# A gated attention/MLP mix on one core: no block and no closing barrier, two gate sums at another place, one output store on another queue

## The chip, the cores and the metric

One core of one Trainium2 chip runs the whole program. The metric is the device time of one launch in microseconds (us), median of several runs; less is better.

## The reference

The input `x` has 2048 rows (positions) of 512 numbers in bfloat16. Two branches are mixed by a gate that is one number per row:

```python
g = sigmoid((x * gate_w).sum(-1, keepdims=True))
# branch A: attention with 32 heads of width 16 over 8 positions, 2 apart
qkv = x @ wqkv
idx = pos[:, None] - 2 * arange(8)[None, :]          # masked where < 0
logits = einsum("bhsd,bhswd->bhsw", q, k[idx]) * 16 ** -0.5
a = einsum("bhsw,bhswd->bhsd", softmax(logits), v[idx]).reshape(B, S, D) @ wo
# branch B: an MLP over the positions
h = layernorm(B_x)
u = gelu(einsum("bsd,sf->bdf", h, w1) + b1)          # F = 1792
b = (einsum("bdf,fs->bds", u, w2) + b2).transpose(0, 2, 1)
out = g * a + (1 - g) * b
```

The kernel uses `x` for both branches and for the gate.

## The kernel before

The kernel is written as a list of named operations. Each has an engine, a function that issues its instructions, an assumed duration, and the tiles that it reads and writes. A list scheduler (`_Sched.schedule`) puts each engine's operations in an order, from assumed durations and dependences, and `plan_waits` gives each operation the semaphore waits that it needs. Where the author wants a certain order, `chain([...])` (near L932) fixes the sequence of the named operations on their engine. Afterwards `emit_engine` (L974 to L994) issues one engine's operations with their waits. At the end of SyncE's list (engine name `sp`) it also waits for the landing of every output store, semaphore by semaphore (L994).

All this stands in `nc.Block()` (L335). A block gives every engine an instruction stream of its own: each engine branches from the main body into its stream (L996 to L1012), and at the end of the block each branches to a common end, where all five engines meet at a barrier. That barrier's instructions carry line 335 in the profile. Ahead of the block, the main body holds four constant fills and an opening barrier (L1028).

The stages that matter here, by engine:

- TensorE (PE): ten warm-up matmuls (L526); the projections to q, k and v (L594); the sums of q times k over the head width (`qkr`, L672); the MLP's first product (`ph2`, L786) and second product (`ph3`, L836); and the product with `wo` (L852). TensorE's list ends with `ph3b_14`, `wo_0` to `wo_3`, `ph3a_15`, `ph3b_15`, then `wo_4` to `wo_15`. The last four output tiles are done in halves of 256 columns.
- VectorE (DVE): layernorm statistics (L549); the products q times k (`qkm`, L664); the 16 gate sums `gz_0` to `gz_15` (L648), each one product with an accumulated sum over one tile of 128 rows; the mask (`msk`, L712); the softmax (`sm_*`, L718 to L751); the products of the attention weights with v and their sums over 8 positions (`avm`, `ava`, `avb`, `avc`: L771, L774, L776); and the final combination of an output tile (`cmb_i`, L873), which reads the `wo` product from PSUM, multiplies it by the gate and adds branch B.
- ScalarE (ACT): evictions of the projections (L602, L605) and of the logits (`lev`, L702), the normalisation (L573), the softmax's exponential (`sm_exp0` and `sm_exp1`, L737), the gelu (L807), the bias copies `b1c` and `b2c` (L517, L518), and branch B's eviction (L903). It also issues 32 transfers that spread the attention weights over the partitions.
- SyncE (SP): issues nearly all other transfers. Tile `i` of the output is stored by `d_out<i>`; tile 15 is stored in halves, the first by SyncE (`d_out15a`) and the second by ScalarE (`d_out15b`, semaphore `d_outb`).

VectorE's order around the softmax is written out by hand. Before the change it is: `gz_12` to `gz_15`, `msk_0`, `sm_ma0`, `sm_mb0`, `gz_0`, `gz_1`, `msk_1`, `sm_ma1`, `sm_mb1`, `sm_m1`, `sm_sub0`, `sm_sub1`, the ten operations from `sm_sa0` to `sm_nrm1`, `gz_2` to `gz_11`, and then `avm_0`. `msk_1` waits for ScalarE's last `lev`; `sm_sa0` waits for `sm_exp0`.

Of the kernel before, what the change touches and what calls it, by code (L numbers as in the profile page):

```python
# [13 lines left out]
D = 512  # L14
# [4 lines left out]
NST = S // 128  # L19
# [313 lines left out]

def bass_gated_mix__sliding_local_dilated__mixer_token_mlp__prompt_kernel(nc, A_x, A_wqkv, A_wo, B_x, B_w1, B_b1, B_w2, B_b2, gate_w, out, dbg=None):
    with contextlib.ExitStack() as es:  # L335
        block = es.enter_context(nc.Block())
        view, pview, off, total = _views(nc, es)
        ps = es.enter_context(nc.psum_tensor("ps", [128, 8, 512], FP32))
        esem = {e: es.enter_context(nc.semaphore("sem_" + e)) for e in ("pool", "act", "dve", "pe")}
        sch = _Sched()  # L340
# [6 lines left out]
        outv = out[0].rearrange("(t p) d -> p t d", p=128)  # L347
# [21 lines left out]
        T1 = view("X", BF16, [(D, NST), (1, D)])  # L369
# [33 lines left out]
        def col(v_, i):  # L403
            return bass.AP(v_.tensor, v_.offset + i, [list(v_.ap[0]), [1, 1]])
# [24 lines left out]
        def mk_dma(dst, src):  # L429
            return lambda e: e.dma_start(dst, src)  # L430
# [115 lines left out]
        for hf in range(2):  # L546
            t0 = 8 * hf
            for t in range(t0, t0 + 8):
                A("dve", (lambda t_: (lambda e: e.bn_stats(out=ST6[:, t_, :], in_=X[:, t_, :])))(t), 0.59,  # L549
                  reads=["x%d" % t], writes=["st6_%d" % t], name="ln1_%d" % t, prio=0)  # L550
# [13 lines left out]
              reads=["zc%d" % hf], writes=["sd%d" % hf], name="ln_sqrt%d" % hf, prio=0)  # L564
            A("dve", (lambda t0_: (lambda e: e.reciprocal(out=cols(RSTD, t0_, 8), in_=cols(SD, t0_, 8))))(t0), 0.25,
              reads=["sd%d" % hf], writes=["rstd%d" % hf], name="ln_rstd%d" % hf, prio=0)
# [43 lines left out]
        for (b0, d0, d1, s0, s1) in ((0, 0, 1, 0, 512), (0, 1, 2, 0, 512), (0, 2, 3, 0, 512), (0, 3, 4, 0, 512), (4, 0, 2, 0, 512), (4, 2, 4, 0, 512)):  # L610
            for b in range(b0, b0 + 4):
                tn, dl = first[b]
                last_main[0] = A("pe", f_proj(tn, dl, 0, b, d0, d1, s0, s1), 0.216 * (d1 - d0) * (s1 - s0) / 512,
                                 reads=ALLXT[s0 // 128:s1 // 128] + ["wqkv%d_%d" % (tn, dt) for dt in range(d0, d1)],
# [11 lines left out]
        for (tn, dl, sb) in seq_proj:  # L626
# [3 lines left out]
                             reads=xr + ["wqkv%d_%d" % (tn, dt) for dt in range(4)],  # L630
# [15 lines left out]
        for t in range(NST):  # L646
# [7 lines left out]
          reads=["th"], writes=["g"], name="g_g", prio=0)  # L654
        A("dve", lambda e: e.tensor_scalar(out=OMG, in0=TH, scalar1=-0.5, scalar2=0.5, op0=ALU.mult, op1=ALU.add), 0.15,
          reads=["th"], writes=["omg"], name="g_omg", prio=0)
        A("dve", lambda e: e.tensor_tensor(out=C2, in0=OMG, in1=B2C, op=ALU.mult), 0.15,
          reads=["omg", "b2c"], writes=["c2"], name="g_c2", prio=0)
# [25 lines left out]
        for wh in range(2):  # L684
# [6 lines left out]
            for (dl, c0, nc_) in pieces:  # L691
# [3 lines left out]
                  reads=["q5_%d_%d" % (dl, sb) for sb in range(c0, c0 + nc_)] +  # L695
# [3 lines left out]
            for wl in range(4):  # L699
                qop = A("pe", f_qkr(list(enumerate(bufs)), (wl,)), 0.92, reads=rd, writes=["lg%d_0" % (4 + wl), "lg%d_1" % (4 + wl)],  # L700
                        name="qkr_%d_%d" % (wh, wl), prio=-100 + wl, delay=BURST_DELAY)
                A("act", (lambda wh_, wl_: (lambda e: e.activation(out=ATT[:, :, 4 * wh_ + wl_, :], in_=ps[:, 4 + wl_, :].rearrange("p (h c) -> p h c", h=2), func=AF.Copy)))(wh, wl),  # L702
                  0.55, reads=["lg%d_0" % (4 + wl), "lg%d_1" % (4 + wl)], writes=["lw%d" % (4 * wh + wl)],
                  name="lev_%d_%d" % (wh, wl), prio=0)
# [24 lines left out]
        for hf in range(2):  # L729
# [3 lines left out]
              reads=["outs1"], writes=["lh%d" % hf] + (wall if hf == 0 else []), name="sm_sub%d" % hf, prio=0)  # L733
            if hf == 0:
                A("act", lambda e: e.activation(out=col(SD, 0), in_=col(ZC, 0), func=AF.Exp, scale=0.0), 1.5,
                  reads=["zc0"], writes=["sd0"], name="sm_pre")
            A("act", (lambda hf_, l_: (lambda e: e.activation(out=ATT[:, hf_], in_=l_, func=AF.Exp)))(hf, lgh), 1.95,  # L737
              reads=["lh%d" % hf], writes=["att%d" % hf], name="sm_exp%d" % hf, prio=0)
        for hf in range(2):
# [5 lines left out]
            def f_rcp(e, hf_=hf):  # L745
# [6 lines left out]
              reads=["rs%d" % hf], writes=["att%d" % hf], name="sm_nrm%d" % hf, prio=0)  # L752
# [4 lines left out]
        for u in range(8):  # L757
            c, hf = u // 2, u % 2
            ds_at = sch.dsem("atx%d" % u)
            for a_ in range(4):  # L760
                dst = bass.AP(ATX.tensor, ATX.offset + a_ * pst + u * NW * HC, [[4 * pst, 32], [1, NW * HC]])
                sch.dma("act", mk_dma(dst, psub(ATT, 32 * c, 32, hf * NW * HC, [(1, NW * HC)])), 32 * NW * HC * 2, ds_at, issue=0.62,
                        reads=["att%d" % hf], writes=["atx_%d_%d" % (u, a_)], deps=pb_readers, name="d_atx_%d_%d" % (u, a_))
        USEQ = [0, 2, 1, 3, 4, 6, 5, 7]
        for k_, u in enumerate(USEQ):
# [6 lines left out]
              reads=v_res + ["atx_%d_%d" % (u, a_) for a_ in range(4)], writes=[pn] + [qk_res, k_all][k_ % 2], name="avm_%d" % u)  # L772
# [30 lines left out]
        for ft in range(NFT):  # L803
# [5 lines left out]
              reads=["acc%d" % bank, "b1c"], writes=["ut%d" % ft] + ALLXT,  # L809
              name="gel_%d" % ft, prio=0)  # L810
# [30 lines left out]
        def WB(i):  # L841
            return (4 + i) % 8

        def WBN(i):
            b_ = WB(i)
            return ["acc%d" % b_] if b_ < 4 else ["lg%d_0" % b_, "lg%d_1" % b_]

        def f_wo(i, bank, c0=0, c1=D):
            def fn(e):
                ins = None  # L850
                for t in range(4):
                    ins = e.matmul(ps[:, bank, 0:c1 - c0], lhsT=OT[:, t, 128 * i:128 * i + 128], rhs=WO[:, t, c0:c1],  # L852
                                   start=(t == 0), stop=(t == 3))
                return ins
            return fn

        ds_out = [sch.dsem("out%d" % k) for k in range(4)]
        ds_outb = sch.dsem("outb")
# [3 lines left out]
        def emit_wo(i):  # L862
            parts = [(0, D)] if i < HT0 else [(0, D // 2), (D // 2, D)]
            ons = []
            for h, (c0, c1) in enumerate(parts):
                k_ = i if len(parts) == 1 else HT0 + 2 * (i - HT0) + h
                bank, bn = WB(k_), WBN(k_)
                sfx = "" if len(parts) == 1 else "ab"[h]
                frac = (c1 - c0) / D
                on = "o%d%s" % (i, sfx)  # L870
                ons.append(on)
                A("pe", f_wo(i, bank, c0, c1), 0.866 * frac, reads=["ot%d" % (i // 2), "wo"], writes=bn, name="wo_%d%s" % (i, sfx), prio=0)
                A("dve", (lambda i_, b_, c0_, c1_: (lambda e: e.scalar_tensor_tensor(  # L873
                    out=T1[:, i_, c0_:c1_], in0=ps[:, b_, 0:c1_ - c0_], scalar=col(G, i_), in1=T1[:, i_, c0_:c1_],
                    op0=ALU.mult, op1=ALU.add)))(i, bank, c0, c1), 0.08 + 0.67 * frac, reads=bn + ["g", "t1_%d" % i], writes=[on],
                  name="cmb_%d%s" % (i, sfx), prio=0)
                if i == NST - 1:
                    q = "act" if sfx == "b" else "sp"
                    sch.dma(q, mk_dma(outv[:, i, c0:c1], T1[:, i, c0:c1]), 128 * (c1 - c0) * 2,
                            ds_out[i % 4] if q == "sp" else ds_outb, issue=0.5, reads=[on], name="d_out%d%s" % (i, sfx))  # L880
            if i < NST - 1:
                sch.dma("sp", mk_dma(outv[:, i, :], T1[:, i, :]), 128 * D * 2, ds_out[i % 4], issue=0.5, reads=ons, name="d_out%d" % i)

        p3bank = {}

# [8 lines left out]
        for i in range(NST):  # L894
# [4 lines left out]
            elif i > 1:  # L899
# [5 lines left out]
              reads=["acc%d" % bank, "omg", "c2"], writes=["t1_%d" % i, "x%d" % i],  # L905
              name="t1_%d" % i, prio=0)
            if i % 2 == 1 and j2 + 3 <= 7:
                ld_w2(j2 + 3)
        for i in range(NST):
            emit_wo(i)  # L910
# [15 lines left out]
        def gz(*ts):  # L926
            return ["gz_%d" % t for t in ts]

        def lnr(hf):
            return ["ln_rstd%d" % hf, "ln_nmr%d" % hf]  # L930
# [1 line left out]
        chain(["rp"] + ln1(0, 1, 2, 3) + ["qkm_0_0_0", "qkm_0_1_0"] + ln1(4, 5, 6, 7) + ln2(0)  # L932
              + ["qkm_0_2_0"] + lnr(0) + ["qkm_0_3_0", "qkm_0_0_2"] + ln1(8, 9) + ["qkm_0_1_2", "qkm_0_2_2", "qkm_0_3_2"] + ln1(*range(10, 16)) + ln2(1)
              + ["t_b", "qkm_1_0_0"] + lnr(1) + ["qkm_1_1_0"]
              + ["qkm_1_2_0", "qkm_1_3_0"] + gz(12, 13, 14, 15) + ["msk_0", "sm_ma0", "sm_mb0"] + gz(0, 1) + [
                 "msk_1", "sm_ma1", "sm_mb1", "sm_m1", "sm_sub0", "sm_sub1"]
              + ["%s%d" % (n_, h_) for h_ in range(2) for n_ in ("sm_sa", "sm_sb", "sm_s1", "sm_rcp", "sm_nrm")] + gz(*range(2, 12))
              + ["%s_%d" % (n_, u) for k_ in range(4) for n_ in ("avm", "ava", "avb", "avc") for u in USEQ[2 * k_:2 * k_ + 2]] + ["cmb_%d" % i for i in range(HT0)] + ["cmb_%d%s" % (i, x_) for i in range(HT0, NST) for x_ in "ab"])
        byname["d_w1_6"].deps.add(byname["d_atx_2_3"])
        chain(["d_w1_3", "d_xb", "d_gw", "d_xa", "d_w1_4", "d_w2_0", "d_w2_1", "d_w1_5", "d_w1_6", "d_w2_2"])  # L940
# [27 lines left out]
        def emit_engine(eng_name, e):  # L968
            for op in sch.order[eng_name]:
                for d in op.waits:  # L970
                    if d.is_dma:
                        e.wait_ge(d.dsem.handle, 16 * d.seq)
                    else:
                        e.wait_ge(esem[d.eng], d.seq)  # L974
                r = op.fn(e)
                if dbg is not None:
                    rr = r[-1] if isinstance(r, list) else r
                    dbg.setdefault("opmap", []).append((eng_name, op.name, rr.ins.name, op.start, op.end))
                if op.is_dma:
                    r.then_inc(op.dsem.handle, 16)  # L980
                elif op.sig:
                    if isinstance(r, list):
                        r = r[-1]
                    r.then_inc(esem[eng_name], 1)
            if eng_name == "sp" and dbg is not None and "keep" in dbg:
                for d in sch.dsems:
                    n_ = len([o for o in sch.ops if o.is_dma and o.dsem is d])
                    if n_ and d.queue == "sp":
                        e.wait_ge(d.handle, 16 * n_)
            if eng_name == OUTQ:  # L990
                for d in ds_out + [ds_outb]:
                    n_ = len([o for o in sch.ops if o.is_dma and o.dsem is d])
                    if n_:
                        e.wait_ge(d.handle, 16 * n_)  # L994

        @block.sync  # L996
        def _(e):
            emit_engine("sp", e)

        @block.gpsimd  # L1000
        def _(e):
            emit_engine("pool", e)

        @block.scalar
        def _(e):
            emit_engine("act", e)

        @block.vector
        def _(e):
            emit_engine("dve", e)  # L1010

        @block.tensor  # L1012
        def _(e):
            emit_engine("pe", e)


# [26 lines left out]
```

## Time and profile before

| | before |
|---|---|
| median of 3 runs | 169.39 us (169.17 to 169.87) |
| profiled execution, its own time | 169.05 us |
| span of the profiled execution, first to last instruction | 167.3 us |
| TensorE busy | 163.2 us |
| VectorE busy | 150.6 us |
| ScalarE busy | 74.7 us |

The span goes from the first instruction of the program to the end of the last one. The execution's own time is longer, since it has the launch around it. In the profile's views, `PEld` is TensorE's weight load, and a `q` behind an engine's name is its sequencer, which waits, branches and issues transfers while the engine may be idle. Matmuls are pipelined, so the busy time of one overlaps that of the next; the time from one start to the next is what a matmul costs.

### The profile page before, as it was taken

What the parts mean: (1) busy time and instruction counts of PE and PEld (TensorE: products, weight loads), DVE (VectorE), ACT (ScalarE), POOL (GpSimd) and SP (SyncE); (2) the same over time, 40 slices, a digit from 0 to 9 for tenths busy, and PEclk for the clock granted to TensorE, in tenths of its full rate; (3) what the DMA queues carried; (4) which work ended last, traced back from release to release, by engine and by line L of the source; (5) the groups of instructions that cost most, each with busy time, mean ns of one, the idle gap of its engine ahead of it and who ended that gap; (6) DMA issues with size and microseconds to landing.
All of it is one profiled execution on the core that took longest, in us unless ns stands there. A gap on an engine that the chain in (4) does not pass through costs nothing.

```text
span 167.3 us, 2153 instructions
## 1 busy us (share of the span) xinstructions
PE 163.2 (98%) x858; PEld 77.6 (46%) x858; DVE 150.6 (90%) x153; ACT 74.7 (45%) x115; POOL 0.7 (0%) x8
## 2 busy tenths in 40 slices
PE   7899999999999999999999999999999999999993
PEld 3455555554554444444444444444444444444462
DVE  0046999998999997799999999999999999999994
ACT  3087698889799818791122311231321312211000
POOL 1000000000000000000000000000000000000000
PEclk9999999999999999999999999999999999999999
DMA  6999999968004856996689926372574370000464
GB/s 149 304 271 258 305 322 290 310 203 233 0 0 122 287 160 164 305 290 148 142 216 338 347 70 156 89 218 83 138 219 126 95 222 0 0 0 0 158 206 142
DMA packets 47609, 29.64 MB, mean 177 GB/s; under 512 B 9840, under 2 KB 46448, under 8 KB 47600
## 3 DMA queue, kind: packets, MB, share of 16 engines
q1 hardware_dynamic: 45776, 25.11, 54.2%
q10 hardware_dynamic: 1824, 4.39, 9.6%
q8 instruction: 7, 0.11, 0.3%
q14 instruction: 2, 0.02, 0.0%
HBM read 21.11 MB, written 2.10 MB: 139 GB/s over the span
## 4 chain that ended last, share of the span: by engine, by line
DVE 57%; PE 35%; DMA 3%; ACT 2%; issue 1%
PE ps L594 25%; DVE arena L771 21%; DVE arena L774 16%; DVE arena L873 7%; PE ps L786 6%; PE ps L672 4%; DVE arena L718 4%; DVE arena L648 4%; DMA arena<-in_A_x_dram 3%; DVE arena L747 2%; DVE arena L776 2%; DVE arena L751 1%; ACT arena L737 1%; DVE arena L732 1%; ACT arena L702 0%
## 5 line engine op out<-in xcount | busy, mean ns | idle before, releaser
L786 PE MATMUL ps<-arena 128*128 128x512 bf16 x224 | 48.7, 379 | 0.0
L836 PE MATMUL ps<-arena 128*128 128x512 bf16 x224 | 48.7, 379 | 0.0
L594 PE MATMUL ps<-arena 128*128 128x512 bf16 x192 | 41.8, 379 | 0.6 <-DMA arena<-in_A_x_dram 0.6
L664 DVE TENSOR_TENSOR arena<-arena 128x4096 bf16<-128x4096 bf16 (+1 forms) x12 | 35.5, 2996 | 1.9 <-ACT arena L605 1.4
L771 DVE TENSOR_TENSOR arena<-arena 128x8192 bf16<-128x8192 bf16 x8 | 35.0, 4419 | 0.0
L786 PEld LDWEIGHTS ps<-arena 128*128 128x128 bf16 x224 | 21.8, 98 | 26.6 <-ACT arena L702 0.4
L836 PEld LDWEIGHTS ps<-arena 128*128 128x128 bf16 x224 | 21.9, 98 | 26.5
L594 PEld LDWEIGHTS ps<-arena 128*128 128x128 bf16 x192 | 21.6, 113 | 20.7 <-issue 1.0
L903 ACT ACTIVATE arena<-ps,arena 128x512 bf16<-128x512 f32 x16 | 12.4, 778 | 39.4 <-PE ps L836 39.4
L774 DVE TENSOR_TENSOR arena<-arena 128x4096 bf16<-128x4096 bf16 (+1 forms) x16 | 27.0, 1751 | 0.0
L605 ACT ACTIVATE arena<-ps 128x512 bf16<-128x512 f32 x32 | 18.6, 596 | 4.7 <-PE ps L594 4.7
L807 ACT ACTIVATE arena<-ps,arena 128x512 bf16<-128x512 f32 x14 | 9.6, 687 | 22.0 <-PE ps L786 15.7
L549 DVE BATCH_NORM_STATS2 arena<-arena 128x6 f32<-128x512 bf16 x16 | 10.0, 680 | 9.1 <-DMA arena<-in_A_x_dram 9.1
L852 PE MATMUL ps<-arena 128*128 128x512 bf16 (+1 forms) x80 | 14.2, 337 | 0.0
L602 ACT ACTIVATE arena<-ps 128x512 bf16<-128x512 f32 x16 | 9.0, 596 | 7.4 <-PE ps L594 7.3
L573 ACT ACTIVATE arena<-arena 128x512 bf16<-128x512 bf16 x16 | 12.2, 807 | 0.0
L873 DVE SCALAR_TENSOR_TENSOR arena<-ps,arena 128x512 bf16<-128x512 f32 (+1 forms) x20 | 11.2, 634 | 0.0
L852 PEld LDWEIGHTS ps<-arena 128*128 128x128 bf16 x80 | 7.8, 98 | 6.2
L648 DVE SCALAR_TENSOR_TENSOR arena<-arena 128x512 bf16<-128x512 bf16 x16 | 10.0, 686 | 0.0
L718 DVE TENSOR_TENSOR arena<-arena 128x512 bf16<-128x512 bf16 (+4 forms) x11 | 7.3, 667 | 1.2 <-ACT arena L737 0.8
L672 PE MATMUL ps<-arena 128*32 128x512 bf16 x128 | 7.3, 380 | 0.0
L702 ACT ACTIVATE arena<-ps 128x512 bf16<-128x512 f32 x8 | 4.7, 593 | 4.6 <-PE ps L672 4.6
(38 smaller groups left out, 39.2 us busy)
## 6 DMA issues: line engine op xcount, KB each, us to landing
arena<-in_B_w_dram SPq DMA_DIRECT2D x7, 1024.0 KB, 8.4
arena<-in_B_w_dram SPq DMA_DIRECT2D x8, 896.0 KB, 5.1
arena<-arena ACTq DMA_DIRECT2D x32, 128.0 KB, 2.9
arena<-in_A_x_dram SPq DMA_DIRECT2D x4, 512.0 KB, 5.3
out_dram<-arena SPq DMA_DIRECT2D x15, 128.0 KB, 1.7
arena<-in_A_x_dram SPq DMA_DIRECT2D x1, 1536.0 KB, 8.1
arena<-in_A_wqkv_dram SPq DMA_DIRECT2D x2, 256.0 KB, 3.6
arena<-in_A_x_dram SPq DMA_DIRECT2D x2, 256.0 KB, 3.6
```

The lines of the kernel that those rows point to most:

```text
L594: ins = e.matmul(ps[:, bank, s0:s1], lhsT=lhsT, rhs=XT[:, dt, sb * 512 + s0:sb * 512 + s1], start=(dt == 0 and s0 == 0), stop=(dt == 3))
L605: return lambda e: e.activation(out=dst, in_=ps[:, bank, :], func=AF.Copy)
L648: A("dve", (lambda s_, t_: (lambda e: e.scalar_tensor_tensor(out=s_, in0=s_, scalar=1.0, in1=GWB, op0=ALU.mult, op1=ALU.mult, accum_out=co ...
L664: return lambda e: e.tensor_tensor(out=PBL[buf][:, :, 512 * c0:512 * (c0 + nc_)], in0=in0, in1=in1, op=ALU.mult)
L672: ins = e.matmul(ps[32 * c:32 * c + 32, 4 + wl, :], lhsT=RP, rhs=PBL[buf][:, wl, c * 512:(c + 1) * 512], start=(dl == 0), stop=(dl == 3), ...
L718: return A("dve", lambda e: e.tensor_tensor(out=o_, in0=a_, in1=b_, op=op_), dur, reads=rd, writes=wr, name=nm)
L771: A("dve", (lambda o_, i0, i1: (lambda e: e.tensor_tensor(out=o_, in0=i0, in1=i1, op=ALU.mult)))(pv, in0, in1), 4.4, reads=v_res + ["atx_% ...
L774: A("dve", (lambda pv_, n__: (lambda e: e.tensor_tensor(out=pv_[:, 0:n__], in0=pv_[:, 0:n__], in1=pv_[:, n__:2 * n__], op=ALU.add)))(pv, n ...
L786: ins = e.matmul(ps[:, bank, :], lhsT=W1W[:, slot, st, 128 * e_:128 * e_ + 128], rhs=X[:, st, :], start=(st == 0), stop=(st == NST - 1))
L836: ins = e.matmul(ps[:, bank, :], lhsT=W2S[slot][:, ft, 128 * e_:128 * e_ + 128], rhs=UT[:, ft, :], start=(ft == 0), stop=(ft == NFT - 1))
L852: ins = e.matmul(ps[:, bank, 0:c1 - c0], lhsT=OT[:, t, 128 * i:128 * i + 128], rhs=WO[:, t, c0:c1], start=(t == 0), stop=(t == 3))
L873: A("dve", (lambda i_, b_, c0_, c1_: (lambda e: e.scalar_tensor_tensor(out=T1[:, i_, c0_:c1_], in0=ps[:, b_, 0:c1_ - c0_], scalar=col(G, i ...
```

## The change

Four things change.

1. `nc.Block()` is gone. All engines' instructions are issued into the main body, after the opening barrier. So the five branches into the block, the branches out of it, and the barrier at its end are gone. SyncE's waits for the output stores stay; they are now the last instructions of the program. The semaphore of SyncE's last wait was carried by the branch out of the block; it now stands on a wait of its own kind, in another pairing: `d_out2`, then `d_out3` with `d_out1`, then `d_outb` with `d_out0`.
2. `gz_2` moves from behind the softmax to the place just ahead of `msk_1`, and `gz_3` to the place between `sm_sub1` and `sm_sa0`.
3. The store of output tile 14 is issued by ScalarE instead of SyncE. It shares the semaphore `d_outb` with the second half of tile 15, ahead of which it stands in ScalarE's order.
4. As the scheduler's assumed times shift, it also puts ScalarE's copy `b1c` (L517) later: behind the fourth `lev` of the first group instead of between two projection evictions.

Nothing that is computed changes, and TensorE's order stays as it was.

```diff
-        block = es.enter_context(nc.Block())
...
             if i < NST - 1:
-                sch.dma("sp", mk_dma(outv[:, i, :], T1[:, i, :]), 128 * D * 2, ds_out[i % 4], issue=0.5, reads=ons, name="d_out%d" % i)
+                q = "act" if i == NST - 2 else "sp"
+                sch.dma(q, mk_dma(outv[:, i, :], T1[:, i, :]), 128 * D * 2, ds_out[i % 4] if q == "sp" else ds_outb, issue=0.5, reads=ons, name="d_out%d" % i)
...
-              + ["qkm_1_2_0", "qkm_1_3_0"] + gz(12, 13, 14, 15) + ["msk_0", "sm_ma0", "sm_mb0"] + gz(0, 1) + [
-                 "msk_1", "sm_ma1", "sm_mb1", "sm_m1", "sm_sub0", "sm_sub1"]
-              + ["%s%d" % (n_, h_) for h_ in range(2) for n_ in ("sm_sa", "sm_sb", "sm_s1", "sm_rcp", "sm_nrm")] + gz(*range(2, 12))
+              + ["qkm_1_2_0", "qkm_1_3_0"] + gz(12, 13, 14, 15) + ["msk_0", "sm_ma0", "sm_mb0"] + gz(0, 1, 2) + [
+                 "msk_1", "sm_ma1", "sm_mb1", "sm_m1", "sm_sub0", "sm_sub1"] + gz(3)
+              + ["%s%d" % (n_, h_) for h_ in range(2) for n_ in ("sm_sa", "sm_sb", "sm_s1", "sm_rcp", "sm_nrm")] + gz(*range(4, 12))
...
-        @block.sync
-        def _(e):
-            emit_engine("sp", e)
...
-        @block.tensor
-        def _(e):
-            emit_engine("pe", e)
+        for eng_name, e in (("sp", nc.sync), ("pool", nc.gpsimd), ("act", nc.scalar), ("dve", nc.vector), ("pe", nc.tensor)):
+            emit_engine(eng_name, e)
```

More of the change, by code (lines that the diff above doesn't have):

```diff
@@ L994, in emit_engine @@
                         e.wait_ge(d.handle, 16 * n_)
-        @block.sync
-        def _(e):
-            emit_engine("sp", e)
-        @block.gpsimd
-        def _(e):
[L1002 to L1010, printed above, removed]
-        @block.tensor
-        def _(e):
-            emit_engine("pe", e)
+        for eng_name, e in (("sp", nc.sync), ("pool", nc.gpsimd), ("act", nc.scalar), ("dve", nc.vector), ("pe", nc.tensor)):
+            emit_engine(eng_name, e)
 _INS = ['A_x', 'A_wqkv', 'A_wo', 'B_x', 'B_w1', 'B_b1', 'B_w2', 'B_b2', 'gate_w']
```

## The prediction

> **What bounds the kernel now.** I read the page first: span, busy times, and the chain that ended last.
>
> ```profile
> span 167.3 us, 2153 instructions
> ...
> PE 163.2 (98%) x858; PEld 77.6 (46%) x858; DVE 150.6 (90%) x153; ACT 74.7 (45%) x115; POOL 0.7 (0%) x8
> ...
> DVE 57%; PE 35%; DMA 3%; ACT 2%; issue 1%
> ```
>
> The two lines disagree. By busy time TensorE (PE) is full; by the chain, VectorE (DVE) carries 57% of the span. The chain is followed back from the last busy instruction and stays on an engine as long as that engine had no gap, so it names one tight path, not the only one. I therefore asked for busy time by stage (columns: length; PE, weight load, DVE, ACT, POOL; clock; DMA), and for TensorE's own rows of the timeline.
>
> ```profile
> 5.10:154.10 149.00, 148.93 (x784) 70.20 (x785) 139.16 (x133) 72.64 (x113) 0.00 (x0) 1.00 0.65 179
> 154.10:164.70 10.60, 10.58 (x65) 6.16 (x63) 10.60 (x20) 0.78 (x1) 0.00 (x0) 1.00 0.47 158
> ```
>
> ```profile
> 147.64 3.62 PE L852 MATMUL ps<-arena 128*128 128x512 bf16 x16
> ...
> 154.11 10.56 PE L852 MATMUL ps<-arena 128*128 128x512 bf16 x64
> ```
>
> ```profile
> L852 PE MATMUL ps<-arena 128*128 128x512 bf16 x48 | 10.7, 379 | 0.0
> ```
>
> ```profile
> 60.82 3.60 PE ps L672 x64
> ```
>
> Busy matmuls overlap, so 148.93 of 149.00 does not yet say full rate. The timeline does: 16 matmuls in 3.62 us, of which the last one's own length is 0.38 (379 ns, by its group's row), make (3.62 - 0.38) / 15 = 0.216 us from start to start. Of the 784 matmuls of the first stretch, 128 are the narrow ones of L672, two groups of 64 with 3.60 us each; the other 656 cost 656 x 0.216 = 141.7, together 148.9 of the 149.0 us. In the last stage 32 full matmuls and 32 of half the columns cost 32 x 0.216 + 32 x 0.108 = 10.4 of the 10.56 us seen, and the rest is what the last one outlasts its slot by. TensorE does not stall there. With a granted clock of 1.00 and no gap from 5.1 us to 164.7 us, nothing that speeds another engine can bring its end forward. VectorE runs as close to the limit beside it. The end of the kernel shows which of the two decides:
>
> ```profile
> 164.19 0.49 PE L852 MATMUL ps<-arena 128*128 128x256 bf16 x3
> ...
> 164.72 0.48 DVE L873 SCALAR_TENSOR_TENSOR arena<-ps,arena 128x256 bf16<-128x256 f32 x1
> 165.23 0.35 ACTq L430 DMA_DIRECT2D out_dram<-arena  x1
> ```
>
> ```profile
> out_dram<-arena ACTq DMA_DIRECT2D x1, 64.0 KB, 1.6
> ```
>
> TensorE's last matmul ends at 164.19 + 0.49 = 164.68. The last combination starts 0.04 us later, at 164.72; it ends at 165.20, ScalarE issues the last store at 165.23, and that lands 1.6 us later, at 166.8. So the order at the end is TensorE, one combination, one store, the tail.
>
> **Part 1: the two gate sums.** VectorE around the softmax, and the sums behind it (from the chain):
>
> ```profile
> 64.31 0.08 DVE L648 DVE_READ_ACCUMULATOR arena<-arena 128x1 f32 x1
> 65.09 0.13 DVE L712 MEMSET arena<- 32x8 bf16 x4 [0.69 <-ACT arena L702]
> 65.25 1.61 DVE L718 TENSOR_TENSOR arena<-arena 128x1024 bf16<-128x1024 bf16 x3
> 66.89 2.36 DVE L732 TENSOR_TENSOR arena<-arena 128x2048 bf16<-128x2048 bf16 x2
> 70.09 2.41 DVE L718 TENSOR_TENSOR arena<-arena 128x1024 f32<-128x1024 bf16 x3 [0.84 <-ACT arena L737]
> ```
>
> ```profile
> 80.92 6.12 DVE arena L648 x20
> ...
> 154.12 11.09 DVE arena L873 x20
> ```
>
> Ten sums, each a product and an accumulator read, cost 6.12 us: 0.61 each. VectorE is idle 0.69 us before `msk_1` (until ScalarE's last logit eviction) and 0.84 us before `sm_sa0` (until the exponential). Each idle stretch takes one sum, with 0.08 and 0.23 us to spare. So `msk_1` and `sm_sa0` start where they did, eight sums stay behind the softmax, and VectorE reaches everything after them 2 x 0.61 = 1.22 us earlier. Bounds: if the sum in the first gap overruns by its accumulator read of 0.08 us, the gain is 1.1 us.
>
> What is late next is TensorE. VectorE's 20 combinations would start near 154.1 - 1.2 = 152.9 us. But the products for tiles 4 to 15 are the last 64 matmuls, which start at 154.11 and run at full rate. VectorE needs 11.1 us for all 20 combinations and starts so early that from about tile 6 on it waits for TensorE. The last combination then starts 0.04 us after the last matmul, exactly as now. Worth at the end: 0.00 us, bounds 0 and -0.04. If TensorE's cover were gone, this part would be worth the whole 1.22.
>
> **Part 2: ScalarE's `b1c`.** It moves behind the first group's last logit eviction, ahead of the first gelu.
>
> ```profile
> 44.94 0.21 ACT L517 ACTIVATE arena<-arena 128x14 f32<-128x14 bf16 x1
> ...
> 57.40 0.69 ACT L807 ACTIVATE arena<-ps,arena 128x512 bf16<-128x512 f32 x1 [0.32 <-PE ps L786]
> ```
>
> It is 0.21 us long, and ScalarE idles 0.32 us for TensorE just before that gelu. One projection eviction queued behind it comes up to 0.21 us later, into an accumulator that TensorE comes back to several matmul groups later. Cost 0.
>
> **Part 3: tile 14 by ScalarE.** In the last stage SyncE is behind:
>
> ```profile
> 162.83 1.10 SPq L430 DMA_DIRECT2D out_dram<-arena  x1
> ...
> 164.45 0.94 SPq L430 DMA_DIRECT2D out_dram<-arena  x2
> ```
>
> The issue of tile 12 took 1.10 us, and the issues of 14 and 15a then stand back to back (0.94 for two). With 14 gone, 15a no longer stands behind it: it is issued when its own combination ends, just as 15b's begins, near 164.75 instead of 164.9. It does not end the kernel, since 15b does. On ScalarE, 14 is issued near 164.4, takes 0.35 (15b's row) to 0.47 us (half of 0.94), and is over before 15b's combination ends at 165.20. Cost of the added issue: 0; if it took 1.10 us like tile 12's, 15b would go out at 165.5, +0.3. I take 0: the issues nearest in time, 14's and 15a's own, are the short ones.
>
> **Part 4: the block.** At the start the chain shows the gap between the opening barrier's release and the first transfer, on which TensorE's first product waits:
>
> ```profile
> 0.74 0.06 issue
> 0.80 4.23 DMA arena<-in_A_x_dram
> ```
>
> The branch into the block lies inside these 0.06 us, so removing it is worth between 0 and 0.06; I take 0.03. [...]
>
> At the end (engine and operation, count, duration in ns, first and last start):
>
> ```profile
> L994 SPq EVENT_SEMAPHORE  x2: 28/28/28, 166.6 to 166.8; - x2
> ```
>
> ```profile
> L335 SPq COMPARE_BRANCH  x1: 33/33/33, 166.9 to 166.9; - x1
> L335 SPq DRAIN  x1: 7/7/7, 167.1 to 167.1; - x1
> ```
>
> SyncE's wait for the last landing ends at about 166.88 (166.8 and some, plus 28 ns). After that come the branch out of the block, a drain, and the gathering and release of five engines, until 167.3: 0.42 us. All of it is on the path, since SyncE is the last to arrive, and all of it goes: in the changed program the wait for `d_outb` is the last instruction. Bounds: if one more wait follows it, 0.05 of the 0.42 stays (166.8 to 166.9 is the distance of two such); if the launch needs a handshake that this barrier provided, all of it comes back.
>
> **Sum.** 0.00 + 0 + 0 - 0.03 - 0.42 = -0.45 us: the span goes from 167.30 to 166.85, and the profiled execution's 169.05 to 168.60, with the 1.75 us outside the span unchanged. The median of the runs lies 0.34 above that execution, so the forecast is 169.39 - 0.45 = 168.94, call it 168.95. Its own range is 168.6 to 169.3 (a median of three runs that spread by 0.7, and 0.05 to 0.1 for the bounds above). A measurement of this kernel can tell some 0.5% from no change, here 0.85 us: faster is below 168.54, slower above 170.24. The forecast lies inside.
>
> **The rivals.** *The chain is right, and VectorE decides the end*: then the 1.22 us reach it, and the time is 169.39 - 0.45 - 1.22 = 167.7. For it speak the 57%; against it the 0.04 us between last matmul and last combination, and the count of TensorE's starts. Chance 0.07.
>
> *The 1.75 us outside shrink.* Without the barrier four engines end early (VectorE's last combination is over at 165.20), while SyncE still waits for the store. If what follows the program is done by each engine for itself, only SyncE's share is left on the path. No row splits the 1.75; if half of them lie behind the end, up to 0.87 us go, and the time is 168.95 - 0.87 = 168.1. Chance 0.22. [...]
>
> *The change does not do what it says*: the launch waits for a meeting of all engines anyway, and costs without the kernel's barrier what it saved. Then only the start's 0.03 is left: 169.35. Chance 0.08. Against it: SyncE arrives last either way, and arrives earlier.
>
> *An instruction fetch lands on the last store* (slower). One did come near the end:
>
> ```profile
> q8 instruction: 1, 0.02, 29.7%
> ```
>
> ```profile
> out_dram<-arena SPq DMA_DIRECT2D x1, 128.0 KB, 3.4
> ```
>
> ```profile
> out_dram<-arena SPq DMA_DIRECT2D x15, 128.0 KB, 1.7
> ```
>
> The first row is a single packet of 16 KB or so between 161.9 and 162.2 us; the store of tile 10, issued at 161.4 and under way then, took 3.4 us where the median is 1.7. Every engine's stream gets shorter, so its fetches shift. If one falls behind 163.5 us, it catches 15b: +1.7 - 0.45, so 170.6. Against it: the stream of TensorE loses a branch, one instruction of some 1,700, so the fetch moves by about one matmul. Chance 0.08.
>
> **How the numbers follow.** Forecast 0.55, within 0.5%; with the rival that nothing changes, 0.63 for the same. Faster: 0.07 + 0.22 = 0.29. Slower: 0.08. The range reaches from 168.0 (the shrinking outside, with 0.1 below it) to 169.8 (the no-gain case plus the upward spread of the runs, about 0.45); it leaves out the first and the last rival, 0.15, and a little of the tails.
>
> **What would show it.** Right: `msk_1` and `sm_sa0` start near 65.1 and 70.1 as now, the first `avm` 1.2 us earlier, VectorE gets gaps in front of combinations from about tile 6, released by TensorE's L852; the last matmul still ends near 164.65, the span ends at SyncE's last wait, near 166.85. Wrong: a last combination 1 us earlier; a TensorE gap after 5.2 us; a time that falls by much more than the span, or not with it.

## The result, and the profile after

| | before | after |
|---|---|---|
| median of 6 runs | 169.63 us (169.06 to 169.90) | 168.31 us (168.18 to 168.81) |
| ratio after / before | | 0.993, 95% interval 0.9906 to 0.9955 |
| profiled execution, its own time | 169.05 us | 168.81 us |
| span of the profiled execution | 167.3 us | 167.5 us |
| time outside the span, profiled execution | 1.75 us | 1.3 us |

The change makes the kernel faster, by 0.7% (0.45% to 0.94%). The profiled execution looks strange at first: its span is 0.2 us *longer* than before, and its time is 0.24 us shorter. Two things are mixed in it, and they have to be taken apart: how TensorE started, and how the program ended.

The page of the changed kernel (up to the output stores, the lines of the code stand one number lower than before):

```profile
span 167.5 us, 2143 instructions
...
PE 164.4 (98%) x858; PEld 77.8 (46%) x858; DVE 150.9 (90%) x153; ACT 74.6 (45%) x115; POOL 0.7 (0%) x8
...
PE 94%; DMA 3%; DVE 2%; issue 0%
...
L872 DVE SCALAR_TENSOR_TENSOR arena<-ps,arena 128x512 bf16<-128x512 f32 (+1 forms) x20 | 11.5, 639 | 0.9 <-PE ps L851 0.7
```

The chain of work that ended last was VectorE for 57% of the span; now it is TensorE for 94%. VectorE has got gaps in its output combinations (0.9 us, most of it until TensorE's `wo` product; the largest, 0.72 us, stands ahead of the sixth), so the chain, followed back from the end, crosses to TensorE and stays there. The two engines were tied before, and the tie is broken.

**The start.** TensorE's first rows, of the kernel before and then of the changed one:

```profile
0.84 3.72 PE L526 MATMUL ps<-const-bfloat16-1.0 128*128 128x512 bf16 x10 [0.84 <-PEq L1028]
5.17 1.02 PE L594 MATMUL ps<-arena 128*128 128x512 bf16 x4 [0.61 <-DMA arena<-in_A_x_dram]
```

```profile
0.84 4.21 PE L525 MATMUL ps<-const-bfloat16-1.0 128*128 128x512 bf16 x10 [0.84 <-PEq L1011]
5.27 2.95 PE L593 MATMUL ps<-arena 128*128 128x512 bf16 x10 [0.23 <-DMA arena<-in_A_x_dram]
```

The same ten warm-up matmuls took 3.72 us in one execution and 4.21 in the other, and the chain shows the first projection stage with it: 32.97 us for 152 matmuls before (first row), 33.60 after (the other rows).

```profile
5.17 32.97 PE ps L594 x152
```

```profile
5.27 33.60 PE ps L593 x152
...
155.02 6.92 PE ps L851 x32
161.94 0.03 issue
161.97 3.98 DVE arena L872 x9
```

The weight loads of the changed kernel, one for each matmul, show the pace of its first projections:

```profile
5.66 0.15 PEld L593 LDWEIGHTS ps<-arena 128*128 128x128 bf16 x1 [0.27 <-issue]
6.08 0.15 PEld L593 LDWEIGHTS ps<-arena 128*128 128x128 bf16 x1 [0.27 <-issue]
6.51 1.45 PEld L593 LDWEIGHTS ps<-arena 128*128 128x128 bf16 x7 [0.27 <-issue]
```

In the first microseconds TensorE starts a 512-column matmul every 0.43 us and then, from one moment on, every 0.216. That moment is not fixed. In the profile before it came during the warm-up, near 4 us (its weight loads start 0.43 us apart up to the one at 3.78, and the next follows at 4.07); in the profile after between 6.5 and 6.8 us, so that some of the real matmuls ran at the slow pace: 33.60 - 32.97 = 0.63 us, and 0.1 from a first load that landed later. TensorE stays 0.74 us behind until the end of its last matmul (165.42 against 164.68). What sets the moment is not shown; the granted clock reads 1.00 in the slow stretch (5.2 to 6.6 us of the changed kernel) and in the quick one behind it (6.6 to 8.0). The change alone does not make the stage slow: the changed kernel with one more wait at TensorE's end has that stage from 5.33 to 38.30 us, 32.97 again. So single profiles differ by up to some 0.6 us in this alone, which is as large as what was to be measured.

**The gate sums.** VectorE around the softmax:

```profile
65.05 0.69 DVE L647 SCALAR_TENSOR_TENSOR arena<-arena 128x512 bf16<-128x512 bf16 x1
65.67 0.08 DVE L647 DVE_READ_ACCUMULATOR arena<-arena 128x1 f32 x1
65.83 0.12 DVE L711 MEMSET arena<- 32x8 bf16 x4
...
69.91 0.68 DVE L647 SCALAR_TENSOR_TENSOR arena<-arena 128x512 bf16<-128x512 bf16 x1
70.52 0.08 DVE L647 DVE_READ_ACCUMULATOR arena<-arena 128x1 f32 x1
70.83 2.41 DVE L717 TENSOR_TENSOR arena<-arena 128x1024 f32<-128x1024 bf16 x3 [0.23 <-ACT arena L736]
...
86.47 8.76 DVE L770 TENSOR_TENSOR arena<-arena 128x8192 bf16<-128x8192 bf16 x2
```

`msk_1` starts at 65.83 (65.09 before) and `sm_sa0` at 70.83 (70.09): both 0.74 us later, which is exactly what TensorE is behind. Each sum sits in its gap, and the second gap has 0.23 us left, the very number of the forecast. The first `avm` starts at 86.47, and before at 86.96:

```profile
86.96 8.76 DVE L771 TENSOR_TENSOR arena<-arena 128x8192 bf16<-128x8192 bf16 x2
```

That is 0.49 earlier in spite of the 0.74, so 1.23 us were gained on VectorE.

**The end.** The last combination, the last store, and SyncE's three waits:

```profile
165.02 0.92 DVE L872 SCALAR_TENSOR_TENSOR arena<-ps,arena 128x256 bf16<-128x256 f32 x2
165.53 0.33 SPq L429 DMA_DIRECT2D out_dram<-arena  x1
165.97 0.34 ACTq L429 DMA_DIRECT2D out_dram<-arena  x1
```

```profile
L994 SPq EVENT_SEMAPHORE  x3: 17/28/28, 165.9 to 167.5; - x3
```

The combination ends at 165.94, the store goes out at 165.97, and SyncE's last wait, which begins to pass at 167.5, is the last instruction. Nothing follows it. Outside the span, the six runs of the changed kernel have 1.27 us on average (time less span), where the profiled execution before had 1.75.

### The profile page after: what moved, and what is told of

It is laid out like the page before. It is cut to its first block, busy times and chain, and to the rows that moved or that the text cites. A ratio compares the mean times of both kernels' runs of the same rounds, so it can differ in the third digit from the quotient of the medians.

```text
span 167.5 us, 2143 instructions
## 1 busy us (share of the span) xinstructions
PE 164.4 (98%) x858; PEld 77.8 (46%) x858; DVE 150.9 (90%) x153; ACT 74.6 (45%) x115; POOL 0.7 (0%) x8
## 4 chain that ended last, share of the span: by engine, by line
PE 94%; DMA 3%; DVE 2%; issue 0%
PE ps L785 29%; PE ps L835 29%; PE ps L593 25%; PE ps L851 6%; PE ps L671 4%; DMA arena<-in_A_x_dram 3%; DVE arena L872 2%
```

## The experiments

All runs are compared with runs of the kernel before on the same chip. "Outside" is time less span.

**1. The block alone.**

```diff
 # the kernel before
-        block = es.enter_context(nc.Block())
...
+        for eng_name, e in (("sp", nc.sync), ...): emit_engine(eng_name, e)
```

> The kernel before with the block and its closing barrier gone, and nothing else changed (gate sums, tile 14 and ScalarE's order as before). Theory 1 (all of the gain lies at the end of the program: 0.42 us of barrier inside the span, and a stretch outside the span that falls from 1.75 to 1.26 us because four engines end while SyncE still waits): the time falls by 0.9 us, to about 168.7 if the runs before are at 169.6, with 1.26 us outside the span. Rival (the gate sums bring part of it): it falls by no more than 0.45 us.

Measured: 168.78 us against 169.76, ratio 0.9934 (0.9911 to 0.9958); outside 1.26 us on average. In its profiled execution TensorE's projections started just as in the one before, so the two can be set side by side:

```profile
5.18 32.97 PE ps L593 x152
...
154.13 11.09 DVE arena L872 x20
```

```profile
L993 SPq EVENT_SEMAPHORE  x3: 17/28/28, 166.3 to 166.8; - x3
```

The first stage takes 32.97 us and the combinations begin at 154.13, as before (32.97 and 154.12). The last wait begins to pass at 166.8 and ends the span at 166.9. The execution took 168.11 us against 169.05: 0.94 less, somewhat over 0.4 of it inside the span and 0.5 outside. By its ratio the block's end alone pays what the whole change pays (0.9934 and 0.993), but each interval is 0.4 us wide to either side, so this alone can't exclude a few tenths from the rest.

**2. The block kept, all else changed.**

```diff
 # the changed kernel
+        block = es.enter_context(nc.Block())
...
+        @block.sync
+        def _(e):
+            emit_engine("sp", e)
...
```

> The changed kernel with the block and its closing barrier put back; gate sums, tile 14 and ScalarE's order stay changed. Theory 1: no change against the kernel before (within 0.1 us once the clock's warm-up is taken out), 1.75 us outside the span, and the last matmul at the same distance from the first projection matmul as before although VectorE's output combinations start 1.2 us earlier. Rival (VectorE sets the end, the gate sums pay): 0.5 to 1.2 us faster than the kernel before.

Measured: 169.26 against 169.76, ratio 0.9972 (0.9957 to 0.9987), outside 1.79 us. So the outside is back. But by these times the rest is not zero: 0.13% to 0.43% faster than before. (What the expectation calls the clock's warm-up is the slow pace of TensorE's first matmuls, 0.43 us each; that a clock causes it is not shown.) Experiments 5 to 7 ask where that comes from.

**3. No block, but a barrier at the end.**

```diff
 # the changed kernel
             emit_engine(eng_name, e)
+        nc.all_engine_barrier()
```

> The changed kernel, still without a block, but with a barrier of all five engines as its last instructions. Theory 1 (what counts is when the engines end): 0.35 to 0.4 us more inside the span behind SyncE's last wait, and the stretch outside the span is back at 1.75 us: together 0.9 us slower than the changed kernel, the same as the kernel before. Rival (the branches and separate instruction streams of the block cost the time outside): the stretch outside stays at 1.26 us, and the time is only 0.35 to 0.4 us above the changed kernel.

Measured: 169.11 against 169.76, ratio 0.997 (0.9954 to 0.9986), outside 1.77 us.

```profile
L998 SPq DRAIN  x1: 7/7/7, 167.5 to 167.5; - x1
L998 SPq EVENT_SEMAPHORE  x1: 17/17/17, 167.7 to 167.7; - x1
...
L998 PEldq EVENT_SEMAPHORE  x1: 51/51/51, 167.7 to 167.7; - x1
```

From SyncE's drain at 167.5 to the end of the span just behind the release, some 0.25 us, where 0.35 to 0.4 were expected: a barrier without the branch in front of it is shorter than the 0.42 of the block's end. The outside is at its old value without any block, so the branches and the separate streams are not what it hangs on.

**4. No barrier, but all engines wait for the last stores.**

```diff
 # the changed kernel
+            if eng_name in ('pool', 'act', 'dve', 'pe'):
+                e.wait_ge(ds_outb.handle, 32)
```

> The changed kernel, no block and no barrier, but GpSimd, ScalarE, VectorE and TensorE each wait at their end for the landing of the same two last output stores that SyncE waits for. All engines then end within about 0.1 us of each other without a barrier. Theory 1 (four engines ending early hides their own end of program): the span ends as in the changed kernel, and the stretch outside is back at 1.75 us, so 0.5 us slower than the changed kernel. Rival (the barrier's own instructions leave something behind that costs outside the span): the stretch outside stays at 1.26 us and the time is that of the changed kernel.

Measured: 168.94 against 169.76, ratio 0.9951 (0.9933 to 0.9969), outside 1.77 us.

```profile
L991 ACTq EVENT_SEMAPHORE  x1: 17/17/17, 167.4 to 167.4; - x1
L991 POOLq EVENT_SEMAPHORE  x1: 17/17/17, 167.4 to 167.4; - x1
L991 DVEq EVENT_SEMAPHORE  x1: 21/21/21, 167.4 to 167.4; - x1
L991 PEldq EVENT_SEMAPHORE  x1: 51/51/51, 167.4 to 167.4; - x1
```

All four pass their wait with SyncE and end there. There is no barrier in this kernel, its span ends where the changed kernel's does, and yet the 0.5 us outside are back. What counts is *when the engines end*. When four of them end while SyncE still waits, 0.5 us less are left behind the span (1.27 against 1.77); the plain reading, which no row of a profile shows, is that this much of what follows the program is done in the shadow of that wait.

**Which engine?** Two single executions, with the same wait on ScalarE and VectorE only, and on TensorE only.

```diff
 # the changed kernel
+            if eng_name in ('act', 'dve'):          # the other kernel: ('pe',)
+                e.wait_ge(ds_outb.handle, 32)
```

> The changed kernel where ScalarE and VectorE also wait at their end for the last two output stores; GpSimd and TensorE still end early. If the 0.5 us outside the span belong to one engine's own end of program, the stretch outside is 1.75 us if it is ScalarE or VectorE, and 1.26 us if it is GpSimd or TensorE.

> The changed kernel where TensorE alone also waits at its end for the last two output stores. The stretch outside the span is 1.75 us if TensorE's own end of program is the long one, 1.26 us if not; a value between says that the engines' ends differ by degrees.

Measured: 168.47 us with a span of 167.1, so about 1.4 outside; and 168.67 with 167.1, so between 1.5 and 1.6. Neither gives the full 1.75, and neither leaves 1.26. TensorE alone costs about half of the half microsecond, ScalarE and VectorE together less. The kernels in which SyncE alone waits went from 1.21 to 1.38 us in their single runs, so the share of ScalarE and VectorE can hardly be told from nothing. GpSimd alone was not tried. That it adds up by degrees rests on one execution each.

**5. and 6. The gate sums alone, tile 14 alone** (block and barrier kept).

```diff
 # the kernel before, 5:
-... + gz(0, 1) + ["msk_1", ..., "sm_sub1"] ... + gz(*range(2, 12))
+... + gz(0, 1, 2) + ["msk_1", ..., "sm_sub1"] + gz(3) ... + gz(*range(4, 12))
 # the kernel before, 6:
+                q = "act" if i == NST - 2 else "sp"
```

> The kernel before, block and barrier kept, with the two gate sums moved and nothing else (the scheduler then also moves ScalarE's small bias copy). With block, gate sums and tile 14 together the span fell by about 0.3 us against the kernel before. Theory A (in many executions VectorE is a little late at the end, though it was not in the profiled one): this kernel takes all of it, 0.2 to 0.3 us faster. Theory B (the gain comes from the store queue at the end, by tile 14): this kernel is the same as before, within 0.1 us.

> The kernel before, block and barrier kept, with output tile 14 stored by ScalarE and nothing else. Theory A (VectorE late): the same as before, within 0.1 us. Theory B (SyncE's stores queue up at the end and hold the last landing): 0.2 to 0.3 us faster.

Measured: the sums alone 169.24 against 169.55, ratio 0.9988 (0.9977 to 0.9999); tile 14 alone 169.15 against 169.55, ratio 0.9979 (0.9967 to 0.9991). Both theories wanted one of them to be zero. By these times tile 14 is worth something, 0.1% to 0.3%; the sums are at the edge of what can be told. Together they were 0.28% in experiment 2, about the sum of the two (0.12% and 0.21%). In neither profile is a late VectorE or a first-half store that lands after `d_out15b`, so the profiles do not show what it is. A rival stands beside it, the moment at which TensorE's pace doubles: it made the first stage 0.63 us longer in one profile than in another, which is more than this. Two more profiles have the same start of TensorE as the two of experiment 1, and so leave it out: tile 14 alone, and the new order of experiment 8 (some matmul records are missing, hence 149):

```profile
5.24 32.97 PE L594 MATMUL ps<-arena 128*128 128x512 bf16 x149 [0.45 <-DMA arena<-in_A_x_dram]
```

```profile
5.25 32.97 PE L594 MATMUL ps<-arena 128*128 128x512 bf16 x149 [0.21 <-DMA arena<-in_A_x_dram]
```

Tile 14 alone has a span of 167.5 us there, against 167.3 for the kernel before; the changed kernel with two extra sums has 167.0, against 166.9 for the block alone. With the same start, neither is shorter. That is one execution each; whether the 0.1% to 0.3% belong to the kernels or to how these moments fell is not settled.

**7. The instruction fetch moved away from the end.** The stores of the end have one visible trouble, a single packet of an instruction queue near 162 us (it starts at 162.1 us in the profile before), which the author took for a fetch by TensorE. More and smaller warm-up matmuls should put it earlier:

```diff
 # the kernel before (and, as a second kernel, the changed one)
-        A("pe", f_warm(9), 3.84, ...
+        A("pe", f_warm(36, 128), 3.84, ...
```

> The kernel before, with TensorE's nine warm-up matmuls of 512 columns cut into 36 of 128 columns: the same warm-up time, but 54 more instructions (27 weight loads, 27 matmuls) ahead of everything, so that TensorE's last instruction fetch, seen at 162.1 us, comes at an earlier place of its work, near 157 to 158 us. Theory B (the fetch blocks the stores, SyncE's issues queue up behind it and hold the last landing in most executions): the issue of tile 12 falls from 0.85 to 1.5 us to 0.35 us, the stores of the end land in 1.6 to 1.7 us, and the time falls by 0.2 to 0.35 us, as with tile 14 alone. Rival (the queue at the end is not what tile 14 changed): no change within 0.1 us.

> The changed kernel with the same cut of the warm-up matmuls, the fetch near 157 to 158 us. Theory B: SyncE's queue is short already, since tile 14 has left it, so only the landing of the last store can gain: 0 to 0.15 us faster than the changed kernel. Rival: 0.2 to 0.35 us faster, if the fetch still held the end in the changed kernel.

The packet moved to 158 us by a change in TensorE's instructions alone, and the queue on SyncE went with it. On the kernel before:

```profile
156.75 5.74 SPq L430 DMA_DIRECT2D out_dram<-arena  x9
```

```profile
158.07 1.46 SPq L430 DMA_DIRECT2D out_dram<-arena  x1
```

```profile
q8 instruction: 1, 0.02, 16.6%
```

The third row is that packet, which now starts between 157.6 and 158.1 us. The first two of the nine stores come ahead of it; the third, issued at 158.07, takes 1.46 us, and the six behind it stand back to back until 162.5. The last ones go out on time. Measured: on the kernel before 169.47 against 169.63, ratio 0.9987 (0.997 to 1.0004); on the changed kernel 168.36, ratio 0.9928 (0.9903 to 0.9953), where the changed kernel had 0.993. So on the changed kernel it does nothing that can be told. On the kernel before the middle value, 0.22 us, is at the low end of theory B, and the interval includes zero. The slowest execution of this kernel before its change had a span of 168.5, with the fetch moved 168.0; that fits a queue that holds the end in some executions, but it isn't shown.

**8. Two more gate sums on VectorE, in the old and in the new order.** This is the direct test of which engine bounds the end.

```diff
 # the changed kernel (for the old order: with the sums back at their old places)
+        for k_ in range(2):
+            A("dve", ... scalar_tensor_tensor(out=JK, in0=XA[:, t_, :], in1=GWB, ..., accum_out=col(JC, t_)) ...)
...
-              ... + gz(*range(4, 12))
+              ... + gz(*range(4, 12)) + ["xtra_0", "xtra_1"]
```

> The changed kernel with the gate sums back at their places of before, and two more sums of the same kind (0.61 us each, their result is not used) on VectorE behind the others. Theory 1 (VectorE has almost no reserve against TensorE in the old order, 0.04 us): 1.1 to 1.25 us slower than the changed kernel, and the chain that ended last runs on VectorE. Rival (TensorE's cover is larger than it looks, VectorE is no bound in either order): no change.

> The changed kernel with its gate sums where the change put them, and the same two more sums on VectorE behind the others (their result is not used). Theory 1 (the move bought VectorE 1.22 us of reserve, which nothing used): the same as the changed kernel within 0.15 us, the end set by TensorE with VectorE 0.04 us behind it. Rival (the move already paid 0.3 us, so VectorE was that late before): 0.2 to 0.4 us slower than the changed kernel.

Measured: old order 169.52 us, new order 168.29 us, against 169.55 for the kernel before in the same runs: ratios 0.9999 (0.9984 to 1.0015) and 0.9929 (0.9913 to 0.9946). The same work at another place is 1.23 us apart. (That the old order comes out at the time of the kernel before is chance: it has no block, which saves time, and two sums more, which cost it.) VectorE's combinations in the chain and TensorE's last matmuls in the timeline of the old order, then the combinations of the new order:

```profile
155.47 11.04 DVE arena L876 x20
```

```profile
164.30 0.38 PE L855 MATMUL ps<-arena 128*128 128x256 bf16 x2
```

```profile
154.33 11.04 DVE arena L876 x20
```

In the old order TensorE is done at 164.30 + 0.38 = 164.68, as before, but VectorE's combinations start 1.35 us later than before (154.12) and end at 166.51: VectorE has become the bound at once, it had no reserve. In the new order the two extra sums fill what the move had freed, the combinations start at 154.33, and the time is that of the changed kernel without them. So the move made 1.2 us of reserve on VectorE, and nothing in the changed kernel uses it.

## Why the prediction was right, and where it was not

The time, 168.31, lies in the range (168.0 to 169.8), and the direction was right. The forecast itself, 168.95, was too high: a ratio of 0.997, outside the measured interval; and the forecast's own range, 168.6 to 169.3, misses the time. That the whole range holds it is owed to the second rival, whose price had set the lower end. The forecast was within 0.5% of no change, and the measured change is more than that by its middle value, though its interval reaches to 0.45%.

- **TensorE bounds the end, and the two sums are worth nothing there.** Right in the profiles. The chain turned to TensorE, the sums filled their gaps with the spare 0.23 us that was forecast, and experiment 8 shows both sides: VectorE's reserve was nil before and 1.2 us after. The first rival (VectorE decides, 167.7) is out. Experiment 5 leaves the sums between nothing and 0.2%.
- **The barrier inside the span, 0.42 us.** Right: in the pair of executions with the same start, the span fell from 167.3 to 166.9, to the forecast 166.85.
- **"with the 1.75 us outside the span unchanged".** This is the step that failed. It fell to 1.27. The second rival had named the mechanism, four engines that end early, with a chance of 0.22 and a price of 0.87; the price measured is 0.5, and experiments 3 and 4 show that it depends on when the engines end and not on the block. With 0.42 + 0.5 the change is worth about 0.9 us, and the matched pair of experiment 1 has 0.94. The rival that all of the barrier's price returns is out. What the time outside is made of, no run shows; 0.5 of the 1.77 us of experiment 4 are gone when four engines end early.
- **The start, 0.03 us.** Not seen: the first transfer is issued at 0.80 us with and without the block, behind a gap of 0.06 us with it and 0.07 without. The profile before has no branch at the start at all; its only one is SyncE's at the block's end, at 166.9 us. So the prediction read a branch into the 0.06 us that the profile does not show, and no run shows the 0.03.
- **Tile 14, 0 us.** Perhaps too small: 0.1% to 0.3% by the times of experiment 6, with the block kept, but nothing in the one profile with the same start. The prediction argued from one execution in which `d_out15b` landed last, and so it does in experiment 6. Whether it pays, and why, stays open.
- **The fetch on the last store.** Did not happen: the packet came 2.6 us ahead of TensorE's end in the profile before (162.1 against 164.68) and 2.3 us ahead in the profile after (163.1 against 165.42).
- **The median.** The medians are 1.32 us apart, where the matched executions are 0.94 apart. Half of the six runs before were at 169.87 to 169.90, one of the six after at 168.81; a slow start of TensorE would give such steps (0.63 us in the profile after), though the runs without a kept trace do not show it, and what is left of the difference is not settled.

## What to carry to other kernels

A program's time does not end with its last instruction (here 1.21 to 1.89 us of a launch lay outside the span): let every engine that is done run to its own end, and let only the engine that must wait for the last store do so; the closing barrier cost 0.42 us of its own instructions here and some 0.5 us outside the span, where no profile row shows it. Before moving work off the engine that the chain names, look whether another engine is just as tight, by its start-to-start times, and test it by adding work instead of removing it. Compare profiled executions only after checking that TensorE's matmuls came to their quick pace (here one in 0.216 us) at the same moment in both.

## What the runs showed of the hardware that was not expected

The ends of the engines seem to overlap by degrees: outside the span were 1.27 us with SyncE alone at the end, about 1.4 with ScalarE and VectorE beside it, 1.5 to 1.6 with TensorE (these two from one execution each), and 1.77 with all five. And a single packet of an instruction queue went with a held-up store. The issue of the store behind it took 1.10 us in the profile before, where the last one took 0.35, and when the packet was moved to 158 us the long issue moved with it (1.46 us at 158.07). The packet took 1.43 us in the profile before and 0.88 in the profile after, and in both the store issue that was held up (the one at 162.83, and the one of 0.85 us at 163.53) ended some 0.4 us after it.
